# Routing attention and a cosine router: x divided while it is turned, routing in column strips, units in pairs

## The chip, the core and the metric

One core of a Trainium2 chip runs the whole kernel. TensorE (PE in the profile; its weight loads are PEld) multiplies and transposes into PSUM, VectorE (DVE), ScalarE (ACT) and GpSimd (POOL) work elementwise, SyncE (SP) issues most transfers. The metric is the device time of one execution in microseconds (us); less is better.

## The reference

Attention over B = 4 batches, H = 8 heads, S = 768 rows, D = 64 columns, in which a query sees only the keys whose nearest of C = 16 centroids is its own:

```python
mask = q_assign[:, :, :, None] == k_assign[:, :, None, :]
scores = np.where(mask, scale * np.matmul(q, k.transpose(0, 1, 3, 2)), -1000000000.0)
attn = np.exp(scores - np.max(scores, axis=-1, keepdims=True))
attn = attn / (np.sum(attn, axis=-1, keepdims=True) + 1e-09)
attn_out = np.matmul(attn, v)
```

Its output, as x of 3072 rows and 512 columns (8 heads side by side), goes to a router over 8 experts. A row's expert is the largest of its cosines with eight embeddings, its weight that expert's softmax, and the expert is two matrices with a relu between:

```python
xn = x / (np.linalg.norm(x, axis=-1, keepdims=True) + 1e-06)
logits = xn @ en.T / tau
expert_idx = np.argmax(logits, axis=1)
h = np.maximum(x[mask] @ w1[e], 0.0)
out[mask] = gate_w[mask, None] * (h @ w2[e])
```

## The kernel before

Heads are worked in 16 pairs (four batches of four). Both heads of a pair stand side by side in the 128 partitions. A pair has 12 units: two halves of the queries (hq, 384 each) times six blocks of 128 keys (j). Six units, one half, are a group: its outputs add up in one PSUM bank.

**A unit.** `scores` (line 326) makes turned scores, keys in partitions and 384 queries in columns, for both heads: first a product of one-hot assignments in bf16 (which adds a very large number where query and key share a centroid), then the fp32 product, each head in its own 64 rows of the array, into one of two `s_ps` buffers. `expo` (342) turns them on ScalarE into `prob` (4 buffers). `attend` (347) multiplies the values with `prob`, each head in its own 64 output columns, into `o_ps`, and VectorE adds `prob` into `acc`, of which the sum over partitions is the softmax's denominator.

**The end of a group.** `evict` (376) copies `o_ps` on ScalarE to `oT`, with a tiny constant `ev` per column added. `finish` (382) takes the denominators with 12 matmuls of one column (lines 391 to 397: six 128x128 pieces of `acc` are loaded as weights, each in two fp32 passes, and meet a column of ones), turns `oT` with three transposes (399), and VectorE divides while it copies to `xr`, x in rows, by reciprocals of 128x6 (401, 405).

**Preparation of the next pair.** `prep_pieces` (206) lists ten pieces: four turns of halves of q and k (three transposes each; q is copied on ScalarE, k on VectorE), products with the centroids (232), their transposes and the largest one per row (`assign`, 245 to 255, the last step on GpSimd), the sum of values (`mean`), the one-hot rows (`choose`, 261 and 262), and their transposes for q and for k (`turn_hot`, 274).

**Routing of a batch.** `route_pieces` (415) has eight pieces: for each of six row blocks four transposes of x (427), a copy on ScalarE, four accumulating matmuls whose moving side is eight columns of embeddings (437), a copy of the logits and a sum of squares (products on GpSimd at 424, the sum on VectorE at 445), and last `choose` (455), some twenty small operations and the transfer of the batch's x with its gate to DRAM (478).

**The order.** Inside the manual schedule (line 487) the program order is the order of TensorE's, VectorE's and ScalarE's queues. One step of the loop is a unit: scores and exponential of unit i + 1, the end of the last group at parts 0 and 1, one piece of preparation, attend of unit i, one piece of routing. All pieces take their PSUM from two banks (`misc`), so a piece also waits until the piece before the last has been copied out.

After the loop come the last batch's routing, the ranking of all rows by expert (lines 530 to 630, its first matmul at 536), and 28 blocks of 128 rows through the experts (633 to 734).

```python
                if i + 1 < len(units):
                    scores(i + 1)
                    expo(i + 1)
                if part == 0 and g > 0:
                    evict(g - 1)
                if part == 1 and g > 0:
                    finish(g - 1)
                if prepare:
                    prepare.pop(0)()
                if i < len(units):
                    attend(i)
                if routing:
                    routing.pop(0)()
```

Of the kernel before, what the change touches and what calls it, by code (L numbers as in the profile page):

```python
# [18 lines left out]
P = 128  # L19
# [16 lines left out]
def kernel(  # L36
# [43 lines left out]
    embT = const.tile([P, KD, E], F32, name="embT")  # L80
    prefc = const.tile([P, C], BF16, name="prefc")
    prefe = const.tile([P, E], BF16, name="prefe")
    ones = const.tile([P, 1], F32, name="ones")
# [20 lines left out]
    with ExitStack() as at:  # L104
# [41 lines left out]
        nc.vector.memset(cnB, 0.0)  # L146
        nc.vector.memset(cumx[:, 0], 0.0)
# [56 lines left out]
        nc.vector.tensor_copy(embT.rearrange("p c e -> p (c e)"), bk[:, 0 : KD * E])  # L204

        def prep_pieces(n):
# [86 lines left out]
            def mean():  # L293
# [10 lines left out]

            return [
                lambda: (turn("q", 0), values()),
                lambda: turn("k", 0),
# [4 lines left out]
                mean,  # L312
                choose,
                lambda: turn_hot(0, "q"),
                lambda: turn_hot(1, "k"),
            ]
# [7 lines left out]
        xr = {}  # L324
# [51 lines left out]
        def evict(g):  # L376
            n = units[GU * g][0]
            d = gr[g]
            d["oT"] = smp.tile([P, HS], F32, tag="oT", name="oT")
            nc.scalar.activation(d["oT"], d["o_ps"][:, 0:HS], ACTF.Identity, bias=ld[n]["ev"])  # L380

        def finish(g):
            n, hq, _ = units[GU * g]
            b, hp = pairs[n]
            d = gr[g]
            U = NJ // 2
            bk = misc()
# [12 lines left out]
            den = smp.tile([P, U, 2], F32, tag="den", name="den")  # L400
            nc.vector.reciprocal(den.rearrange("p u h -> p (u h)"), bk[:, HS : HS + 2 * U])  # L401
            if b not in xr:
                xr[b] = xp.tile([P, NJ, XW], F32, tag="xr", name="xr")
# [11 lines left out]
        def route_pieces(b):  # L415

            t = {}

            def turn(j):
                if j == 0:  # L420
                    t["sq"] = smp.tile([P, NJ], F32, tag="sq", name="sq")
                    t["lg"] = smp.tile([P, NJ, E], F32, tag="lg", name="lg")
                junk = smp.tile([P, DM], F32, tag="junk", name="junk")
                nc.gpsimd.tensor_tensor(junk, xr[b][:, j, 0:DM], xr[b][:, j, 0:DM], ALU.mult)  # L424
                bk = misc()
                for c in range(KD):
                    nc.tensor.transpose(  # L427
                        bk[:, P * c : P * c + P], xr[b][:, j, P * c : P * c + P], ident
                    )
                t[j] = trp.tile([P, DM], F32, tag="xT", name="xT")  # L430
                nc.scalar.copy(t[j], bk)
                t["junk", j] = junk

            def logits(j):
                bk = misc()
                for c in range(KD):
                    nc.tensor.matmul(  # L437
                        bk[:, 0:E],
# [339 lines left out]
```

## Time and profile before

| what | us |
|---|---|
| median of 3 runs | 970.41 (968.58 to 971.48) |
| profiled execution, its own time | 971.72 |
| its span, first to last instruction | 969.8 |
| PE busy in the span | 916.4 (94%) |
| DVE busy | 296.9 (31%) |
| ACT busy | 285.4 (29%) |
| POOL busy | 157.6 (16%) |

The span is what the rows of the profile lie in; 1.9 us of the profiled execution lie around it. A busy share is a mean over stages with different limits, so the stages are read apart. A line of the timeline gives the start, the time until the last of its instructions ended, engine, line, operation, tiles, shapes and count; on PE the starts are the safer reading, since the ends are modelled. An fp32 matmul is recorded as two passes, so `x4` at line 354 is one attend: two heads, two passes.

### The profile page before, as it was taken

How to read it: one execution, taken by the hardware profiler on the slowest of the kernel's cores; microseconds unless marked ns; L12 is line 12 of the kernel's file. 1: busy time of each engine (PE TensorE's matmuls, PEld its weight loads, DVE VectorE, ACT ScalarE, POOL GpSimd, SP SyncE). 2: the span in 40 equal slices, each digit the busy share in tenths (PEclk: the TensorE clock that was granted, in tenths of full speed). 3: DMA queues.
4: the chain of work that ended last, by engine and by line, in shares of the span. 5: the costliest groups of instructions: out<-in, count | busy, mean ns of one | idle time of the engine just before them, and what ended most of it. 6: DMA issues, size and time to landing. Idle time of an engine off the chain costs nothing.

```text
span 969.8 us, 13780 instructions
## 1 busy us (share of the span) xinstructions
PE 916.4 (94%) x5663; PEld 545.8 (56%) x5663; DVE 296.9 (31%) x527; ACT 285.4 (29%) x421; POOL 157.6 (16%) x195
## 2 busy tenths in 40 slices
PE   4999999999999999999996499999999999999996
PEld 2444446344464444544445477776776776776773
DVE  2545555554555546464553300000000000000000
ACT  3444443544445444444432011111111111111110
POOL 4011022201131111311012301011011011111110
PEclk9999999999999999999995599999999999999998
DMA  9722201420114111220000226256766573813710
GB/s 248 264 50 49 49 18 33 115 49 22 45 33 114 27 40 33 50 82 17 1 1 1 98 85 247 98 205 223 262 219 230 191 280 142 288 44 115 287 33 19
DMA packets 105648, 106.91 MB, mean 110 GB/s; under 512 B 77157, under 2 KB 77157, under 8 KB 105072
## 3 DMA queue, kind: packets, MB, share of 16 engines
q1 hardware_dynamic: 100928, 92.30, 30.1%
q0 software_dynamic: 4480, 13.65, 3.8%
q8 instruction: 47, 0.77, 0.3%
q14 instruction: 17, 0.14, 0.0%
q10 hardware_dynamic: 176, 0.05, 0.0%
HBM read 152.11 MB, written 13.64 MB: 171 GB/s over the span
## 4 chain that ended last, share of the span: by engine, by line
PE 48%; issue 25%; DMA 19%; DVE 5%; ACT 2%; POOL 1%; POOLq 0%; ACTq 0%; DVEq 0%
DMA out_dram<-y,sidx 19%; PE s_ps L334 16%; PE o_ps L354 14%; PE misc L391 5%; PE misc L217 3%; PE misc L437 3%; PE misc L427 2%; PE misc L274 1%; PE misc L232 1%; PE misc L399 1%; DVE oh L262 1%; PE misc L245 1%; DVE xr L405 1%; DVE pm L261 1%; DVE acc L373 1%
## 5 line engine op out<-in xcount | busy, mean ns | idle before, releaser
L345 ACT ACTIVATE prob<-s_ps 128x768 f32<-128x768 f32 x192 | 155.4, 811 | 245.1 <-PE s_ps L334 243.6
L682 PEld LDWEIGHTS h_ps<-xTm,w1s 128*128 128x128 f32 x1792 | 204.5, 193 | 19.9 <-DVE xTm L672 15.7
L682 PE MATMUL h_ps<-xTm,w1s 128*128 128x128 f32 x1792 | 208.6, 278 | 0.9 <-DMA w1s<-in_moe_w_dram 0.9
L695 PE MATMUL y_ps<-w2s,hT 128*128 128x512 f32 x448 | 201.2, 592 | 0.0
L354 PE MATMUL o_ps<-prob,v 128*64 128x384 f32 x768 | 166.3, 512 | 4.7 <-ACT prob L345 4.5
L334 PE MATMUL s_ps<-qT,kT 64*128 64x384 f32 x768 | 156.5, 486 | 0.0
L672 DVE COPY xTm<-x_ps 128x512 f32<-128x512 f32 x28 | 19.4, 691 | 378.4 <-PE x_ps L670 378.4
L373 DVE TENSOR_TENSOR acc<-acc,prob 128x768 f32<-128x768 f32 x128 | 125.3, 979 | 17.6 <-ACT prob L345 11.3
L695 PEld LDWEIGHTS y_ps<-w2s,hT 128*128 128x128 f32 x448 | 81.0, 190 | 81.3 <-issue 81.3
L689 ACT ACTIVATE hT<-h_ps 128x512 f32<-128x512 f32 x56 | 33.4, 597 | 240.5 <-PE h_ps L682 240.5
L704 POOL DMA_INDIRECT out_dram<-y,sidx x28 | 28.5, 1017 | 353.6 <-ACT y L703 347.7
L334 PEld LDWEIGHTS <-kH 64*128 64x128 bf16 x384 | 18.5, 93 | 103.4 <-issue 101.9
L334 PEld LDWEIGHTS s_ps<-qT,kT 64*128 64x128 f32 x768 | 70.2, 192 | 0.5 <-issue 0.5
L354 PEld LDWEIGHTS o_ps<-prob,v 128*64 128x64 f32 x768 | 38.0, 134 | 55.0 <-issue 36.3
L334 PE MATMUL s_ps<-qH,kH 64*128 64x384 bf16 x384 | 64.9, 335 | 0.9 <-ACT kH L282 0.9
L703 ACT ACTIVATE y<-y_ps,xin 128x512 f32<-128x512 f32 x28 | 19.2, 688 | 137.8 <-PE y_ps L695 131.6
L391 PEld LDWEIGHTS misc<-ones,acc 128*128 128x128 f32 x384 | 45.3, 191 | 17.9 <-issue 15.2
L391 PE MATMUL misc<-ones,acc 128*128 128x1 f32 x384 | 48.0, 252 | 0.4 <-DVE acc L373 0.4
L401 DVE RECIPROCAL den<-misc 128x6 f32<-128x6 f32 x32 | 6.3, 196 | 131.6 <-PE misc L399 131.6
L288 POOL TENSOR_TENSOR vs<-v 128x384 f32<-128x384 f32 x16 | 16.0, 998 | 187.7 <-DMA v<-in_v_dram 168.2
L424 POOL TENSOR_TENSOR junk<-xr 128x512 f32<-128x512 f32 x24 | 29.0, 1217 | 90.8 <-DVE sq L445 50.9
L255 POOL TENSOR_TENSOR sel<-sel,prefc 128x384 bf16<-128x384 bf16 x16 | 24.3, 1518 | 119.1 <-DVE sel L254 114.0
(144 smaller groups left out, 606.5 us busy)
## 6 DMA issues: line engine op xcount, KB each, us to landing
w1s<-in_moe_w_dram SPq DMA_DIRECT2D x30, 2048.0 KB
w2s<-in_moe_w_dram SPq DMA_DIRECT2D x30, 2048.0 KB
x_rows<-xr SPq DMA_DIRECT2D x4, 1539.0 KB
q<-in_q_dram SPq DMA_DIRECT2D x32, 192.0 KB
k<-in_k_dram SPq DMA_DIRECT2D x32, 192.0 KB
v<-in_v_dram SPq DMA_DIRECT2D x32, 192.0 KB
xin<-x_rows,gidx POOLq DMA_INDIRECT x28, 7.6
out_dram<-y,sidx POOLq DMA_INDIRECT x28, 7.8
```

Source lines behind the costliest of these rows:

```text
L217: nc.tensor.transpose(bk[:, P * j : P * j + P], t[nm][:, NJ // 2 * half + j].rearrange("p h d -> p (h d)"), ident,)
L334: nc.tensor.matmul(s_ps[:, h, 0:HS], lhsT=t[l][rows, P * j : P * j + P], rhs=t[r][rows, HS * hq : HS * hq + HS], start=first, stop=not first,)
L345: nc.scalar.activation(d["prob"], d["s_ps"][:, :, 0:HS], ACTF.Exp)
L354: nc.tensor.matmul(g["o_ps"][D * h : D * h + D, 0:HS], lhsT=ld[n]["v"][:, j, h], rhs=d["prob"][:, h], start=(j == 0), stop=(j == NJ - 1),)
L373: nc.vector.tensor_tensor(g["acc"], g["acc"], d["prob"], ALU.add)
L391: nc.tensor.matmul(bk[:, c0 : c0 + 1], lhsT=d["acc"][:, h, P * u : P * u + P], rhs=ones, start=True, stop=True,)
L424: nc.gpsimd.tensor_tensor(junk, xr[b][:, j, 0:DM], xr[b][:, j, 0:DM], ALU.mult)
L437: nc.tensor.matmul(bk[:, 0:E], lhsT=t[j][:, P * c : P * c + P], rhs=embT[:, c], start=(c == 0), stop=(c == KD - 1),)
L682: nc.tensor.matmul(bk[:, m : m + P], lhsT=w1s[j % 2][:, c, f0 + m : f0 + m + P], rhs=d["xT"][:, P * c : P * c + P], start=(c == 0), stop=( ...
L689: nc.scalar.activation(d["hT"][:, f0 : f0 + 512], bk, ACTF.Relu)
L695: nc.tensor.matmul(bk, lhsT=d["hT"][:, P * c : P * c + P], rhs=w2s[j % 2][:, c], start=(c == 0), stop=(c == KF - 1),)
L704: nc.gpsimd.indirect_dma_start(out=out[:], out_offset=bass.IndirectOffsetOnAxis(ap=sidx[:, j : j + 1], axis=0), in_=y, in_offset=None, bou ...
```

## The change

The ones that sum `acc` become a 128x64 matrix, so that one product per head (`total`) puts the denominator of each query into all 64 partitions of the head's output: it comes out turned, in the shape of `o_ps`. ScalarE copies it, VectorE takes the reciprocal of all 128x384 and multiplies it with `o_ps + ev` in one instruction into `xT`, x turned and divided (`divide`). Two parts later `rows` turns three blocks back and ScalarE copies them to `xr`. The router multiplies the turned x directly: four column strips (pairs of heads) times a 128x32 embedding each (8 columns and 24 of zeros) into the four quarters of one bank, then three transposes and one reduction over the strips. Squares are summed on ScalarE. The loop takes two units at a time: scores of two, a piece of preparation, attend of two, the sum and division of the last group at part 0, another piece of preparation, a piece of routing; the exponentials run a whole step ahead. Preparation has nine pieces, the first turns both q and k. `prob` has five buffers.

The diff, without the changes of sizes and of the embedding's copy at the top:

```diff
@@ -302,17 +305,17 @@
                 t["ev"] = smp.tile([P, 1], F32, tag="ev", name="ev")
                 nc.vector.tensor_copy(t["ev"], bk[:, 0:1])
 
+
             return [
-                lambda: (turn("q", 0), values()),
-                lambda: turn("k", 0),
+                lambda: (turn("q", 0), turn("k", 0), values()),
                 lambda: turn("q", 1),
                 lambda: turn("k", 1),
                 products,
                 assign,
-                mean,
                 choose,
                 lambda: turn_hot(0, "q"),
                 lambda: turn_hot(1, "k"),
+                mean,
             ]
 
 
@@ -321,7 +324,7 @@
         ngroups = len(units) // GU
         un = [dict() for _ in units]
         gr = [dict() for _ in range(ngroups)]
-        xr = {}
+        xr, xT = {}, {}
 
         def scores(i):
 
@@ -341,7 +344,7 @@
 
         def expo(i):
             d = un[i]
-            d["prob"] = pp.tile([P, 2, HS], F32, tag="prob", name="prob", bufs=4)
+            d["prob"] = pp.tile([P, 2, HS], F32, tag="prob", name="prob", bufs=5)
             nc.scalar.activation(d["prob"], d["s_ps"][:, :, 0:HS], ACTF.Exp)
 
         def attend(i):
@@ -373,84 +376,96 @@
                 nc.vector.tensor_tensor(g["acc"], g["acc"], d["prob"], ALU.add)
                 d.clear()
 
-        def evict(g):
-            n = units[GU * g][0]
+        def total(g):
+
             d = gr[g]
-            d["oT"] = smp.tile([P, HS], F32, tag="oT", name="oT")
-            nc.scalar.activation(d["oT"], d["o_ps"][:, 0:HS], ACTF.Identity, bias=ld[n]["ev"])
-
-        def finish(g):
+            bk = misc()
+            for h in range(2):
+                nc.tensor.matmul(
+                    bk[D * h : D * h + D, 0:HS],
+                    lhsT=ones,
+                    rhs=d["acc"][:, h],
+                    start=True,
+                    stop=True,
+                )
+            d["den"] = smp.tile([P, HS], F32, tag="den", name="den")
+            nc.scalar.copy(d["den"], bk[:, 0:HS])
+
+        def divide(g):
             n, hq, _ = units[GU * g]
             b, hp = pairs[n]
             d = gr[g]
+            if (b, hq) not in xT:
+                xT[b, hq] = xp.tile([P, NHP, HS], F32, tag="xT", name="xT", bufs=3)
+            nc.vector.reciprocal(d["den"], d["den"])
+            nc.vector.scalar_tensor_tensor(
+                out=xT[b, hq][:, hp],
+                in0=d["o_ps"][:, 0:HS],
+                scalar=ld[n]["ev"],
+                in1=d["den"],
+                op0=ALU.add,
+                op1=ALU.mult,
+            )
+            d.clear()
+
+        def rows(g):
+
+            n, hq, _ = units[GU * g]
+            b, hp = pairs[n]
             U = NJ // 2
             bk = misc()
             for u in range(U):
-                for h in range(2):
-                    c0 = HS + 2 * u + h
-                    nc.tensor.matmul(
-                        bk[:, c0 : c0 + 1],
-                        lhsT=d["acc"][:, h, P * u : P * u + P],
-                        rhs=ones,
-                        start=True,
-                        stop=True,
-                    )
-            for u in range(U):
-                nc.tensor.transpose(bk[:, P * u : P * u + P], d["oT"][:, P * u : P * u + P], ident)
-            den = smp.tile([P, U, 2], F32, tag="den", name="den")
-            nc.vector.reciprocal(den.rearrange("p u h -> p (u h)"), bk[:, HS : HS + 2 * U])
+                nc.tensor.transpose(
+                    bk[:, P * u : P * u + P], xT[b, hq][:, hp, P * u : P * u + P], ident
+                )
             if b not in xr:
                 xr[b] = xp.tile([P, NJ, XW], F32, tag="xr", name="xr")
-            c0 = 2 * D * hp
-            nc.vector.tensor_tensor(
-                xr[b][:, U * hq : U * hq + U, c0 : c0 + 2 * D].rearrange(
-                    "p u (h d) -> p u h d", d=D
-                ),
-                bk[:, 0:HS].rearrange("p (u h d) -> p u h d", h=2, d=D),
-                bc(den, [P, U, 2, D], 3),
-                ALU.mult,
-            )
-            d.clear()
+            nc.scalar.copy(
+                xr[b][:, U * hq : U * hq + U, P * hp : P * hp + P],
+                bk[:, 0:HS].rearrange("p (u w) -> p u w", w=P),
+            )
 
         def route_pieces(b):
 
             t = {}
-
-            def turn(j):
-                if j == 0:
+            U = NJ // 2
+
+            def products(half):
+
+                if half == 0:
                     t["sq"] = smp.tile([P, NJ], F32, tag="sq", name="sq")
                     t["lg"] = smp.tile([P, NJ, E], F32, tag="lg", name="lg")
-                junk = smp.tile([P, DM], F32, tag="junk", name="junk")
-                nc.gpsimd.tensor_tensor(junk, xr[b][:, j, 0:DM], xr[b][:, j, 0:DM], ALU.mult)
-                bk = misc()
-                for c in range(KD):
-                    nc.tensor.transpose(
-                        bk[:, P * c : P * c + P], xr[b][:, j, P * c : P * c + P], ident
-                    )
-                t[j] = trp.tile([P, DM], F32, tag="xT", name="xT")
-                nc.scalar.copy(t[j], bk)
-                t["junk", j] = junk
-
-            def logits(j):
                 bk = misc()
                 for c in range(KD):
                     nc.tensor.matmul(
-                        bk[:, 0:E],
-                        lhsT=t[j][:, P * c : P * c + P],
-                        rhs=embT[:, c],
-                        start=(c == 0),
-                        stop=(c == KD - 1),
-                    )
-                nc.vector.tensor_copy(t["lg"][:, j], bk[:, 0:E])
+                        bk[2 * C * c : 2 * C * c + 2 * C, 0:HS],
+                        lhsT=embT[:, c],
+                        rhs=xT[b, half][:, c],
+                        start=True,
+                        stop=True,
+                    )
+                t["pT"] = smp.tile([P, HS], F32, tag="asT", name="asT")
+                nc.scalar.copy(t["pT"], bk[:, 0:HS])
+
+            def logits(half):
+                bk = misc()
+                for u in range(U):
+                    nc.tensor.transpose(
+                        bk[:, P * u : P * u + P], t["pT"][:, P * u : P * u + P], ident
+                    )
                 nc.vector.tensor_reduce(
-                    t["sq"][:, j : j + 1], t["junk", j], axis=AXX, op=ALU.add
+                    t["lg"][:, U * half : U * half + U],
+                    bk[:, 0:HS].rearrange("p (u c e) -> p u e c", c=KD, e=2 * C)[:, :, 0:E],
+                    axis=AXX,
+                    op=ALU.add,
                 )
 
-            def both(j):
-                if j < NJ:
-                    turn(j)
-                if j > 0:
-                    logits(j - 1)
+            def norms(half):
+                for j in range(U * half, U * half + U):
+                    junk = smp.tile([P, DM], F32, tag="junk", name="junk")
+                    nc.scalar.activation(
+                        junk, xr[b][:, j, 0:DM], ACTF.Square, accum_out=t["sq"][:, j : j + 1]
+                    )
 
             def choose():
                 lg, sq = t["lg"], t["sq"]
@@ -480,7 +495,13 @@
                     in_=xr[b],
                 )
 
-            return [lambda j=j: both(j) for j in range(NJ + 1)] + [choose]
+            return [
+                lambda: products(0),
+                lambda: (logits(0), norms(0)),
+                lambda: products(1),
+                lambda: (logits(1), norms(1)),
+                choose,
+            ]
 
 
         prepare, routing = [], []
@@ -488,9 +509,12 @@
             for piece in prep_pieces(0):
                 if piece:
                     piece()
-            scores(0)
-            expo(0)
-            for i in range(len(units) + 2):
+            for m in range(2):
+                scores(m)
+                expo(m)
+
+
+            for i in range(0, len(units) + 6, 2):
                 g, part = divmod(i, GU)
                 if i < len(units) and i % (2 * NJ) == 0:
                     n = i // (2 * NJ)
@@ -507,23 +531,26 @@
                             nc.sync.dma_start(
                                 out=w2s[w], in_=moe_w2[0].rearrange("(c p) d -> p c d", p=P)
                             )
-                if i + 1 < len(units):
-                    scores(i + 1)
-                    expo(i + 1)
-                if part == 0 and g > 0:
-                    evict(g - 1)
-                if part == 1 and g > 0:
-                    finish(g - 1)
+                for m in range(i + 2, min(i + 4, len(units))):
+                    scores(m)
+                    expo(m)
                 if prepare:
                     prepare.pop(0)()
-                if i < len(units):
-                    attend(i)
+                if part == 4 and g > 0:
+                    rows(g - 1)
+                for m in range(i, min(i + 2, len(units))):
+                    attend(m)
+                if part == 0 and g > 0:
+                    total(g - 1)
+                    divide(g - 1)
+                if prepare:
+                    prepare.pop(0)()
                 if routing:
                     routing.pop(0)()
-                if part == 1 and g > 0 and g % (2 * NHP) == 0 and g < ngroups:
+                if part == 4 and g > 0 and g % (2 * NHP) == 0:
                     assert not routing
                     routing = route_pieces(g // (2 * NHP) - 1)
-            for piece in route_pieces(B - 1):
+            for piece in routing:
                 piece()
```

## Rows read from the trace of the kernel before

**Rows 1.** Busy time by stage: us, engines (instructions), granted clock, DMA share, GB/s

```profile
20.90:506.40 485.50, 476.58 (x3156) 225.84 (x3156) 252.36 (x414) 219.50 (x314) 80.41 (x95) 1.00 0.21 57
506.40:547.70 41.30, 19.32 (x115) 17.90 (x113) 18.13 (x54) 7.12 (x11) 13.00 (x14) 0.54 0.13 48
```

**Rows 2.** Timeline of the pair from 77.5 us, PE and two others

```profile
77.50 0.34 PE L334 MATMUL s_ps<-qH,kH 64*128 64x384 bf16 x2
...
78.41 0.87 PE L354 MATMUL o_ps<-prob,v 128*64 128x384 f32 x4
78.53 0.81 ACT L345 ACTIVATE prob<-s_ps 128x768 f32<-128x768 f32 x1 [0.84 <-PE s_ps L334]
...
82.30 1.50 PE L391 MATMUL misc<-ones,acc 128*128 128x1 f32 x12
...
83.66 0.53 PE L399 MATMUL misc<-ident,oT 128*128 128x128 f32 x3
...
84.02 0.49 PE L217 MATMUL misc<-ident,k 128*128 128x128 f32 x3
...
90.53 0.52 PE L232 MATMUL misc<-qT,cnB 128*32 128x384 f32 x2
...
91.31 0.87 PE L354 MATMUL o_ps<-prob,v 128*64 128x384 f32 x4
...
100.43 0.56 DVE L262 TENSOR_TENSOR oh<-sel,pm 128x384 bf16<-128x384 bf16 x1
...
101.05 0.51 PE L274 MATMUL misc<-identb,oh 128*128 128x128 bf16 x6 [0.23 <-DVE oh L262]
...
105.35 0.87 PE L354 MATMUL o_ps<-prob,v 128*64 128x384 f32 x4
...
106.15 0.34 PE L334 MATMUL s_ps<-qH,kH 64*128 64x384 bf16 x2
```

**Rows 3.** Timeline of PE at the start of the loop

```profile
20.95 0.50 PE L334 MATMUL s_ps<-qH,kH 64*128 64x384 bf16 x2 [0.89 <-ACT kH L282]
...
22.52 0.53 PE L334 MATMUL s_ps<-qH,kH 64*128 64x384 bf16 x2
```

**Rows 4.** Timeline of PE, first scores of pairs 4, 5 and 6

```profile
135.34 0.34 PE L334 MATMUL s_ps<-qH,kH 64*128 64x384 bf16 x2
...
172.37 0.34 PE L334 MATMUL s_ps<-qH,kH 64*128 64x384 bf16 x2
...
202.61 0.34 PE L334 MATMUL s_ps<-qH,kH 64*128 64x384 bf16 x2
```

**Rows 5.** Groups by line and shape, DVE: busy us, mean ns | idle before

```profile
L373 DVE TENSOR_TENSOR acc<-acc,prob 128x768 f32<-128x768 f32 x128 | 125.3, 979 | 17.6 <-ACT prob L345 11.3
...
L405 DVE TENSOR_TENSOR xr<-misc,den 128x384 f32<-128x384 f32 x32 | 17.9, 558 | 1.1
...
L471 DVE RECIPROCAL sq<-sq 128x6 f32<-128x6 f32 x4 | 0.8, 192 | 0.1
...
L182 DVE RECIPROCAL cn_r<-cn_r 128x1 f32<-128x1 f32 x1 | 0.2, 163 | 0.0
...
L182 DVE RECIPROCAL en_r<-en_r 8x1 f32<-8x1 f32 x1 | 0.1, 148 | 0.0
```

**Rows 6.** The same view, ACT

```profile
L240 ACT COPY asT<-misc 128x384 f32<-128x384 f32 x16 | 7.7, 480 | 2.5 <-PE misc L232 2.4
...
L469 ACT ACT_TABLE_LOAD x4 | 5.1, 1283 | 0.1
```

**Rows 7.** Timeline of PE, the last attend and the ranking's first matmul

```profile
505.70 0.20 PEld L354 LDWEIGHTS o_ps<-prob,v 128*64 128x64 f32 x4 [0.79 <-ACT prob L345]
...
529.69 0.33 PE L536 MATMUL misc<-cumx,onesb 128*128 128x200 bf16 x1 [3.57 <-POOL cumx L468]
```

**Rows 8.** Line 363: count, duration in ns (min/median/max), first and last start

```profile
L363 DVE SCALAR_TENSOR_TENSOR acc<-prob x32: 947/950/1791, 27.7 to 500.4; 128x768 f32<-128x768 f32 x32
```

More of the change, by code (lines that the diff above doesn't have):

```diff
@@ L79 @@
     cnB = const.tile([P, NHP, 2 * C], F32, name="cnB")
-    embT = const.tile([P, KD, E], F32, name="embT")
+    embT = const.tile([P, KD, 2 * C], F32, name="embT")
     prefc = const.tile([P, C], BF16, name="prefc")
     prefe = const.tile([P, E], BF16, name="prefe")
-    ones = const.tile([P, 1], F32, name="ones")
+    ones = const.tile([P, D], F32, name="ones")
     epsc = const.tile([P, 1], F32, name="epsc")
@@ L146 @@
         nc.vector.memset(cnB, 0.0)
+        nc.vector.memset(embT, 0.0)
         nc.vector.memset(cumx[:, 0], 0.0)
@@ L203 @@
             nc.tensor.transpose(bk[:, E * c : E * c + E], emb[:, P * c : P * c + P], ident[0:E, 0:E])
-        nc.vector.tensor_copy(embT.rearrange("p c e -> p (c e)"), bk[:, 0 : KD * E])
+        nc.vector.tensor_copy(
+            embT[:, :, 0:E], bk[:, 0 : KD * E].rearrange("p (c e) -> p c e", e=E)
+        )
         def prep_pieces(n):
@@ L388, in finish, with route_pieces @@
             for u in range(U):
-                for h in range(2):
-                    c0 = HS + 2 * u + h
+                nc.tensor.transpose(
+                    bk[:, P * u : P * u + P], xT[b, hq][:, hp, P * u : P * u + P], ident
+                )
+            if b not in xr:
+                xr[b] = xp.tile([P, NJ, XW], F32, tag="xr", name="xr")
+            nc.scalar.copy(
+                xr[b][:, U * hq : U * hq + U, P * hp : P * hp + P],
+                bk[:, 0:HS].rearrange("p (u w) -> p u w", w=P),
+            )
+        def route_pieces(b):
+            t = {}
+            U = NJ // 2
+            def products(half):
+                if half == 0:
+                    t["sq"] = smp.tile([P, NJ], F32, tag="sq", name="sq")
+                    t["lg"] = smp.tile([P, NJ, E], F32, tag="lg", name="lg")
+                bk = misc()
+                for c in range(KD):
                     nc.tensor.matmul(
-                        bk[:, c0 : c0 + 1],
-                        lhsT=d["acc"][:, h, P * u : P * u + P],
-                        rhs=ones,
+                        bk[2 * C * c : 2 * C * c + 2 * C, 0:HS],
+                        lhsT=embT[:, c],
+                        rhs=xT[b, half][:, c],
                         start=True,
@@ L397, in finish @@
                     )
-            for u in range(U):
-                nc.tensor.transpose(bk[:, P * u : P * u + P], d["oT"][:, P * u : P * u + P], ident)
-            den = smp.tile([P, U, 2], F32, tag="den", name="den")
-            nc.vector.reciprocal(den.rearrange("p u h -> p (u h)"), bk[:, HS : HS + 2 * U])
-            if b not in xr:
-                xr[b] = xp.tile([P, NJ, XW], F32, tag="xr", name="xr")
-            c0 = 2 * D * hp
-            nc.vector.tensor_tensor(
-                xr[b][:, U * hq : U * hq + U, c0 : c0 + 2 * D].rearrange(
-                    "p u (h d) -> p u h d", d=D
-                ),
-                bk[:, 0:HS].rearrange("p (u h d) -> p u h d", h=2, d=D),
-                bc(den, [P, U, 2, D], 3),
-                ALU.mult,
-            )
@@ L432, in turn @@
-                t["junk", j] = junk
-            def logits(j):
-                bk = misc()
-                for c in range(KD):
-                    nc.tensor.matmul(
-                        bk[:, 0:E],
-                        lhsT=t[j][:, P * c : P * c + P],
-                        rhs=embT[:, c],
-                        start=(c == 0),
-                        stop=(c == KD - 1),
-                    )
-                nc.vector.tensor_copy(t["lg"][:, j], bk[:, 0:E])
-                nc.vector.tensor_reduce(
-                    t["sq"][:, j : j + 1], t["junk", j], axis=AXX, op=ALU.add
-                )
@@ L449, in both @@
-            def both(j):
-                if j < NJ:
-                    turn(j)
-                if j > 0:
-                    logits(j - 1)
+                nc.vector.tensor_reduce(
+                    t["lg"][:, U * half : U * half + U],
[8 more added lines that the diff above has]
+                        junk, xr[b][:, j, 0:DM], ACTF.Square, accum_out=t["sq"][:, j : j + 1]
+                    )
```

4 lines of the change are left out of this document (removed).

## The prediction

> **What bounds the kernel now.** I read the stage table first [rows 1]. From 20.9 to 506.4 us (attention) TensorE is busy 476.6 of 485.5 us while VectorE has 252 and ScalarE 219.5; after 547.7 us stands the expert stage, which the change does not touch. So the question is what TensorE's queue does between 21 and 506 us, and how long the thin stretch to 547.7 takes, where TensorE was granted 0.54 of its clock.
>
> The timeline of one head pair comes next [rows 2]; its 12 units take 106.15 - 77.50 = 28.65 us. A unit's scores (S) start at 77.50, its attend (A) follows at 78.41: 0.91 us. From A at 105.35 to the next S: 0.80. S streams 0.16 us of bf16 and 0.64 of fp32 columns, A streams 0.64, so each leaves a gap behind it: 0.11 after S, 0.16 after A. The gap is not there when S follows S: at the start of the loop, where matmuls run at about half the speed (a record of 0.50 us against 0.34), S at 20.95 is followed by S at 22.52, 1.57 us, no more than twice its 0.80 of columns [rows 2, 3]. A directly behind A without another wait is not in the trace. I take the gap as the price of changing the shape of the array's tiles, paid once per run of one shape.
> The Trainium skill, TensorEngine Tiling (Array Packing), Key Properties, says that a change of tiling mode, not of the tile alone, drains the engine; by it A behind A would save its gap too, which no row here shows.
>
> A group (six units) ends with 12 one-column matmuls, 1.36 us (82.30 to 83.66), and three transposes, 0.36 [rows 2]. Routing a batch costs 37.03 + 30.24 - 2 x 28.65 = 9.97 us, over two pairs [rows 4], three times in the loop.
>
> **Part by part, per pair, on TensorE.**
> (a) Two units at a time: six SS and six AA instead of twelve of each save 6 x 0.11 + 6 x 0.16 = 1.62 us.
> (b) Group ends: before 2 x (1.36 + 0.36) = 3.44. After, the sum by the matrix of ones has A's tile shape and columns and stands right behind A: 2 x 0.64 = 1.28. The row transposes: 2 x 0.36 and one gap of 0.14, the other shared with the assignment's transposes (0.14 is what products lose, 0.78 against 0.64 of columns, 90.53 to 91.31 [rows 2]): 2.14 in all. Saves 1.30.
> (c) q and k of half 0 are turned together: about 0.2 less in gaps.
> Sum: 3.12 us less work per pair.
>
> (d) What the change adds is VectorE's reciprocal of 128x384, and its price is the unknown. The trace has RECIPROCAL of 6 elements at 192 ns and of one at 163 (128 partitions) and 148 ns (8 partitions) [rows 5]. The slope is 5.8 ns an element from the first, 8.8 from the second, 7.3 from their mean: 384 x 7.3 + 148 = 2.95 us, with ends at 2.4 and 3.5. I take 2.95; the operation is the same and neither end is nearer.
> The Trainium skill, VectorE: DVE Perf Modes, First, the fixed hardware budget, says that the reciprocal is an iterative divide with a repeat count of 8; at that page's 0.96 GHz it is by my estimate 3.35 us, which would make the sum below 7 us longer.
>
> (e) Who waits behind it. Set t = 0 at a pair's first S. SS 1.71, six transposes 0.84, AA 1.28, sum 0.64: to 4.47. A hand-over from TensorE takes 0.23 (S at 77.50 and 0.80 of columns, its exponential at 78.53), one from VectorE 0.06 (oh ends 100.99, its transposes start 101.05) [rows 2]. The copy on ScalarE, 0.48 [rows 6], ends at 5.18; reciprocal 5.24 to 8.19; the product with it, 0.56 as L405 [rows 5], to 8.78; only then, in VectorE's order, the copy of k's second half, to 9.26. The centroid products need that copy. TensorE reaches them at 4.47 + 0.16 + q 0.46 + SS 1.71 + k 0.48 + AA 1.44 = 8.72 and waits to 9.32: 0.60 us. Below 2.35 us of reciprocal this wait is gone.
> Products 0.78 and SS 1.71 bring TensorE to 11.81, the assignment's transposes to 12.17; two steps of 0.56 on VectorE to 13.55, two accumulations of 0.98 [rows 5] to 15.5 (they cover the GpSimd step between), two more of 0.56 to 16.55. The one-hot transposes want that result; TensorE is there at 12.65 + AA 1.44 + SS 1.71 = 15.80: 0.80 us of wait. Before, the same place cost 0.23 [rows 2].
> Per pair: 28.65 - 0.23 - 3.12 + 1.40 = 26.70, a saving of 1.95; 16 pairs 31, less 1 for the first, which has no group end ahead of it: **30 us**.
>
> (f) Routing. After: two products of 0.78, two sets of three transposes at 0.46, 2.5 us; the chain of some eleven small VectorE operations at about 0.2 us (as L471 [rows 5]) delays the next one-hots by some 1.4, other waits 0.2: 4.1 against 9.97. Three batches: **17.5 us**.
>
> (g) After the last attend. Before: the last A starts at 505.70, its columns end at 506.35, and the ranking matmul starts at 529.69 [rows 7]: 23.3 us. After: VectorE has four accumulations queued behind the last reciprocal but one, so the last sum starts about 2.2 us on; sum and copy to 3.6, reciprocal and product to 7.2, row transposes and products at half the clock to 9.3, copy and transposes to 10.8, three squares ahead of the second half's copy on ScalarE to 12.8, transposes and reduction to 14.4, choice 1.2, GpSimd's counts 1.6: 17.3. **6 us** saved.
>
> Sum: 53.5 us. The profiled execution took 971.7 (span 969.8), the median of the runs is 970.4; I take the 53.5 from the median: **917 us**.
>
> **Costed at nothing.** On ScalarE the copies of sums, rows and products (32, 32 and 8, at 0.48 [rows 6]) are 35 us and the 24 squares, at an estimated 0.7, 17 us: with what it has, 219.5 + 52 of 485.5 us [rows 1], and a unit's exponential now has a whole step of about 4 us until its attend; without that lead three squares in a row, some 2 us, would hold an attend. If the squares needed another table set, each batch half would pay two loads of 1.28 us [rows 6]: hidden in the loop, at most 5 us in the tail. Fifth prob buffer, third turned x, padded embedding: no instruction on a chain. x_rows goes out one pair later in SP's queue, behind the next pair's loads instead of ahead of them; those are a whole pair early. GpSimd loses its 24 products.
>
> **The rivals.** *Hidden reciprocal* (2.4 us or less): no wait at products, 16 x 0.6 and 0.6 in the tail: 907. For it: the slope from 128 partitions. *Dear reciprocal* (3.5): 0.58 more each time: 927; for it the other slope. *The gap is not of the shape*, so each S and A keeps it: 1.62 and 0.3 (the sums) come back, and the waits shrink by 0.55: 1.4 x 16, 939. Against it stands S behind S [rows 3], for it that A behind A is not seen. *VectorE becomes the bound, slower*: an accumulation of the same queue took 1.79 us instead of 0.95 [rows 8], and the long ones have GpSimd work beside them. Were every reciprocal stretched as much, to 5.9 us, the wait at products would grow by 1.35 up to a reciprocal of 4.3, and from there the row transposes of the second group wait too, two waits a pair: 17 x 1.35 + 33 x 1.6 = 76, 993 us. It decides from 5.2 us on (23 + 33 x 0.9 uses up the 53.5), 13 ns an element. Against it: GpSimd is busy 80 us in 485 [rows 1] and loses its largest product.
>
> **How the numbers follow.** Forecast 0.42, hidden 0.18, dear 0.20, gaps stay 0.15, VectorE bound 0.05. From 901 (hidden, with a little less wait at the one-hots) to 941 (gaps stay) all but the last and some unforeseen are in. Faster by over 0.3% (about what a measurement here tells from none) 0.95, slower 0.04, same 0.01.
>
> **What would show it.** Right: RECIPROCAL 128x384 near 2.95 us; S starts 0.80 apart inside a step and A 0.64; TensorE waits of 0.6 at products for kT and 0.8 at the one-hots for oh; pairs of 26.7 us; ranking some 17 us after the last A. Wrong: a reciprocal over 4.3 us, an A behind A at 0.80, exponentials that wait for prob, attends that wait for ScalarE.

## The result and the profile after

The changed kernel takes **923.9 us** (median of 4 runs, 923.1 to 926.4) against 970.9 for the kernel before on the same chip: ratio 0.951 [0.947, 0.956], 47 us faster. The forecast was 917 with a range of 901 to 941: direction and size held, 6.5 us of the 53.5 did not come. The profiled execution took 926.4 us, its span is 924.4 (before 969.8), so the two profiles differ by 45.4 us.

By stage, after: us, then busy time (instructions) of PE, PEld, DVE, ACT and POOL, granted clock, DMA share, GB/s. The first two rows answer to [rows 1]; the last three are stretches inside the first.

```profile
19.40:465.70 446.30, 420.01 (x2759) 192.86 (x2758) 314.35 (x383) 235.40 (x369) 55.05 (x75) 0.98 0.23 63
465.70:505.00 39.30, 12.09 (x73) 6.88 (x72) 19.14 (x47) 8.62 (x20) 8.91 (x10) 0.54 0.17 61
178.70:182.20 3.50, 3.50 (x16) 1.39 (x15) 1.42 (x2) 0.00 (x0) 0.00 (x0) 0.51 0.01 4
291.40:298.20 6.80, 6.14 (x28) 2.94 (x30) 2.71 (x5) 0.97 (x2) 0.00 (x0) 0.50 0.08 31
407.40:410.80 3.40, 3.40 (x12) 1.05 (x12) 1.42 (x2) 0.00 (x0) 0.00 (x0) 0.51 0.00 0
```

Attention went from 485.5 to 446.3 us. TensorE's idle time rose from 8.9 to 26.3 us in it, and VectorE is busy 62 us longer: TensorE's busy time fell by 56.6 us, the stage by only 39.2. New, behind the start of the loop, are three stretches in which TensorE got 0.50 of its clock, 1.2 instead of 2.4 GHz; before, this part of the stage ran at 1.00.

One pair on TensorE, after (timeline; start us, duration us, line; answers to [rows 2]):

```profile
73.00 0.34 PE L337 MATMUL s_ps<-qH,kH 64*128 64x384 bf16 x2
...
73.82 0.33 PE L337 MATMUL s_ps<-qH,kH 64*128 64x384 bf16 x2
...
74.72 0.55 PE L418 MATMUL misc<-ident,xT 128*128 128x128 f32 x3
75.19 1.51 PE L357 MATMUL o_ps<-prob,v 128*64 128x384 f32 x8
76.64 0.34 PE L337 MATMUL s_ps<-qH,kH 64*128 64x384 bf16 x2
...
80.50 0.81 PE L384 MATMUL misc<-acc,ones 128*64 128x384 f32 x4
81.25 0.55 PE L220 MATMUL misc<-ident,q 128*128 128x128 f32 x3
...
85.36 0.52 PE L235 MATMUL misc<-qT,cnB 128*32 128x384 f32 x2
...
86.36 0.34 PE L337 MATMUL s_ps<-qH,kH 64*128 64x384 bf16 x2
...
91.15 0.33 PE L337 MATMUL s_ps<-qH,kH 64*128 64x384 bf16 x2
...
93.38 0.51 PE L277 MATMUL misc<-identb,oh 128*128 128x128 bf16 x6 [1.26 <-DVE oh L265]
...
99.82 0.34 PE L337 MATMUL s_ps<-qH,kH 64*128 64x384 bf16 x2
```

A pair without routing (a plain pair in what follows) is 99.82 - 73.00 = 26.82 us (28.65 before). S follows S by 0.82 us. Two attends go from 75.19 to 76.64, 1.45 in all: 0.70 for A behind A (that is their distance in the trace), 0.75 for S behind A. The products last from 85.36 to 86.36, 1.00 us where they took 0.78 [rows 2]: 0.22 is the wait for k's second half. The one-hot transposes wait 1.26 us.

The same pair on VectorE and one row of GpSimd (timeline), and the reciprocal's group (busy us, mean ns):

```profile
81.88 2.55 DVE L400 RECIPROCAL den<-den 128x384 f32<-128x384 f32 x1 [1.18 <-ACT den L392]
84.46 0.62 DVE L401 SCALAR_TENSOR_TENSOR xT<-o_ps,ev,den 128x384 f32<-128x384 f32 x1
85.00 0.55 DVE L229 COPY kT<-misc 128x384 f32<-128x384 f32 x1
85.46 1.94 DVE L376 TENSOR_TENSOR acc<-acc,prob 128x768 f32<-128x768 f32 x2
...
89.73 2.53 DVE L376 TENSOR_TENSOR acc<-acc,prob 128x768 f32<-128x768 f32 x2
89.90 1.55 POOL L258 TENSOR_TENSOR sel<-sel,prefc 128x384 bf16<-128x384 bf16 x1 [7.06 <-DVE sel L257]
...
92.76 0.56 DVE L265 TENSOR_TENSOR oh<-sel,pm 128x384 bf16<-128x384 bf16 x1
```

```profile
L400 DVE RECIPROCAL den<-den 128x384 f32<-128x384 f32 x32 | 81.7, 2553 | 46.8 <-ACT den L392 46.8
```

The reciprocal is 2.55 us. The copy of k's second half stands behind it, as the prediction had it. Of the two runs of two accumulations, the second takes 2.53 us instead of 1.94: there GpSimd's product of `sel` (1.55 us from 89.90) runs beside them, and the one-hots stand behind.

A routed pair on TensorE and VectorE (timeline):

```profile
171.72 0.22 DVE L485 TENSOR_SCALAR sq<-sq 128x6 f32<-128x6 f32 x1 [0.37 <-ACT sq L484]
...
173.27 0.20 DVE L490 TENSOR_REDUCE mx<-lg 128x6 f32<-128x48 f32 x1 [0.74 <-ACT lg L489]
...
173.99 0.34 PE L337 MATMUL s_ps<-qH,kH 64*128 64x384 bf16 x2 [0.43 <-ACT prob L348]
...
178.49 0.62 PE L277 MATMUL misc<-identb,oh 128*128 128x128 bf16 x6 [2.71 <-DVE oh L265]
179.04 2.83 PE L357 MATMUL o_ps<-prob,v 128*64 128x384 f32 x8
```

Here the twelve small VectorE operations of the choice (170.22 to 173.91 us) make the one-hots wait 2.71 us, and then two attends take 2.83 us instead of 1.51: the half clock in the third row of the stage table. For 0.37 + 0.74 = 1.11 us of this chain VectorE itself waits, for the choice's square root and exponential on ScalarE, with a table load of 1.28 us ahead of each (the loads were there before the change too; no run leaves them out).

The tail, after the last attend (timeline; answers to [rows 7]):

```profile
465.01 0.81 PE L357 MATMUL o_ps<-prob,v 128*64 128x384 f32 x4
467.92 0.87 PE L384 MATMUL misc<-acc,ones 128*64 128x384 f32 x4 [2.09 <-DVE acc L376]
...
472.76 0.87 PE L418 MATMUL misc<-ident,xT 128*128 128x128 f32 x3 [3.98 <-DVE xT L401]
...
482.70 0.33 PE L563 MATMUL misc<-cumx,onesb 128*128 128x200 bf16 x1 [3.19 <-POOL cumx L483]
```

The last attend's first pass starts at 465.01, the ranking at 482.70: 17.7 us, against 24.0 [rows 7].

**Where the 45.4 us came from**, forecast and measured:

| part | forecast | measured | worked out from |
|---|---|---|---|
| start of the loop | 0 | 1.5 | first S at 19.42 instead of 20.95; 19.4 to 21.0 over all runs |
| pairs without their routing | 30 | 27.9 | 14 x 1.83, and 1.14 each in the first and last |
| routing in the loop | 17.5 | 11.3 | before 3 x 10.45 over plain pairs; after 6.27, 7.49, 6.33 |
| last attend to ranking | 6 | 6.3 | 24.0 and 17.7 |
| ranking to the end | 0 | -1.5 | 440.1 and 441.7 (unrounded: 1.54 apart); 438.6 to 443.0 in the eight other runs with as many expert tiles |

### The profile page after: what moved, and what is told of

Same layout as the page of the kernel before. It is cut to its first block, busy times and chain, and to the rows that moved or that the text cites. A ratio compares the mean times of both kernels' runs of the same rounds, so it can differ in the third digit from the quotient of the medians.

```text
span 924.4 us, 12733 instructions
## 1 busy us (share of the span) xinstructions
PE 847.7 (92%) x5207; PEld 497.6 (54%) x5207; DVE 358.7 (39%) x488; ACT 302.8 (33%) x485; POOL 127.9 (14%) x171
## 4 chain that ended last, share of the span: by engine, by line
PE 39%; issue 28%; DMA 19%; DVE 10%; ACT 2%; POOL 1%; SPq 0%; POOLq 0%; DVEq 0%
DMA out_dram<-y,sidx 18%; PE s_ps L337 15%; PE o_ps L357 13%; DVE acc L376 4%; PE misc L220 3%; PE misc L384 2%; PE misc L235 2%; PE misc L277 2%; DVE oh L265 1%; PE misc L418 1%; DVE sel L257 1%; DVE amax L256 1%; PE misc L440 1%; DVE pm L264 1%; PE misc L248 1%
## 5 line engine op out<-in xcount | busy, mean ns | idle before, releaser
L348 ACT ACTIVATE prob<-s_ps 128x768 f32<-128x768 f32 x192 | 153.4, 811 | 89.9 <-PE s_ps L337 67.7
L699 DVE COPY xTm<-x_ps 128x512 f32<-128x512 f32 x28 | 19.4, 691 | 379.7 <-PE x_ps L697 379.7
L357 PE MATMUL o_ps<-prob,v 128*64 128x384 f32 x768 | 148.9, 510 | 0.0
L376 DVE TENSOR_TENSOR acc<-acc,prob 128x768 f32<-128x768 f32 x128 | 130.2, 1017 | 5.8
L400 DVE RECIPROCAL den<-den 128x384 f32<-128x384 f32 x32 | 81.7, 2553 | 46.8 <-ACT den L392 46.8
L357 PEld LDWEIGHTS o_ps<-prob,v 128*64 128x64 f32 x768 | 47.3, 138 | 50.3 <-issue 48.7
L337 PEld LDWEIGHTS <-kH 64*128 64x128 bf16 x384 | 19.4, 94 | 58.2 <-issue 44.2
L392 ACT COPY den<-misc 128x384 f32<-128x384 f32 x32 | 15.3, 479 | 85.8 <-PE misc L384 85.8
L277 PE MATMUL misc<-identb,oh 128*128 128x128 bf16 x192 | 16.9, 227 | 27.2 <-DVE oh L265 27.2
L229 DVE COPY kT<-misc 128x384 f32<-128x384 f32 x32 | 17.7, 553 | 51.4 <-PE misc L220 51.4
```

The costliest lines, as they stand in the source:

```text
L277: nc.tensor.transpose(bk[:, P * j : P * j + P], oh[:, u, 2 * i + half].rearrange("p h c -> p (h c)"), identb,)
L337: nc.tensor.matmul(s_ps[:, h, 0:HS], lhsT=t[l][rows, P * j : P * j + P], rhs=t[r][rows, HS * hq : HS * hq + HS], start=first, stop=not first,)
L357: nc.tensor.matmul(g["o_ps"][D * h : D * h + D, 0:HS], lhsT=ld[n]["v"][:, j, h], rhs=d["prob"][:, h], start=(j == 0), stop=(j == NJ - 1),)
L376: nc.vector.tensor_tensor(g["acc"], g["acc"], d["prob"], ALU.add)
L400: nc.vector.reciprocal(d["den"], d["den"])
```

## The experiments

First the parts of the change, then the reciprocal, then what the loop still waits for.

**Old routing (e2).** The changed kernel with the routing of before (per row block four transposes, four matmuls of eight columns, and squares on GpSimd), shortened:

```
-                nc.tensor.matmul(bk[...], lhsT=embT[:, c], rhs=xT[b, half][:, c], ...)
+                nc.tensor.transpose(bk[...], xr[b][:, j, P * c : P * c + P], ident)
...
+                nc.gpsimd.tensor_tensor(junk, xr[b][:, j, 0:DM], xr[b][:, j, 0:DM], ALU.mult)
```

> The kernel after with the routing of before (turn x in rows again, four matmuls of eight columns per row block, squares on GpSimd and VectorE); loop, group ends and preparation as after, two buffers of turned x. Theory (the strips take work off TensorE's chain): a routed batch costs about 10 us in the loop instead of 6.7, and after the last attend the old pieces take some 12 us longer than the new: about 945 us. Rival (TensorE waits in those pairs anyway, so old routing pieces fill the waits): the loop's pairs cost the same and only the end is longer, 932 to 936 us.

942.3 us, ratio 0.968 [0.964, 0.973]. Plain pairs stay at 26.83 us; each batch's routing costs 8.3 us over plain pairs, and the last attend to the ranking takes 12.9 us longer than in the changed kernel. So the strips are worth 18.4 us, 12.9 of it in the tail and only 5 in the loop. Two things make the loop's part small: the changed kernel has its three stretches at half the clock there, e2 has none; and the old routing fills one wait of 1.26 us a batch (the pair from 155.8 us has no wait at the one-hots). That units two at a time alone make the old routing cheaper than its 10.45 is not shown: with the old group ends it costs 9.7 to 12.9 us a batch in e3 and 12.5 to 15.6 in e8, losses by the clock included.

**Units one at a time (e4).** The changed kernel with the order S, A, S, A, each S still a whole step ahead of its attend (shortened; the conditions at the loop's end are left out):

```
-                for m in range(i, min(i + 2, len(units))):
-                    attend(m)
+                attend(i)
+                scores(i + 3); expo(i + 3)
+                attend(i + 1)
```

> The kernel after with its two units taken in turn (S, A, S, A) while the exponentials keep their lead and all else stays in place. Theory (gap of the tile shape): each S and A leaves its gap again, 12 more gaps a pair, six of 0.10 and six of 0.08 to 0.16, of which the waits at products and one-hots swallow about a third: 12 to 18 us more, 936 to 942 us. Rival (the lead is what gains): within 3 us of 924.

946.5 us, 22.6 more than the changed kernel where 12 to 18 were expected: a plain pair is 27.90 instead of 26.83, some 16 us over the loop. Between the two profiled executions there are 19.9 us, and what is left of them lies at the loop's start (1.2), in the routing (1.5) and behind the ranking (1.2). TensorE (timeline):

```profile
77.25 0.34 PE L337 MATMUL s_ps<-qH,kH 64*128 64x384 bf16 x2
...
78.16 0.87 PE L357 MATMUL o_ps<-prob,v 128*64 128x384 f32 x4
78.96 0.34 PE L337 MATMUL s_ps<-qH,kH 64*128 64x384 bf16 x2
...
82.39 0.87 PE L357 MATMUL o_ps<-prob,v 128*64 128x384 f32 x4
83.08 0.82 PE L384 MATMUL misc<-acc,ones 128*64 128x384 f32 x4
```

S to A is back at 0.91 and A to S at 0.80, while the sum, which has other operands and another bank but A's tile shape, follows A by 0.69. So the gap comes with the change of shape; the rival that every S and A keeps it falls. That the lead of the exponentials is what gains falls too, for this run has that lead.

**Pairing alone (e3).** The kernel before with the new loop and order of pieces, group ends and routing left as they were (shortened):

```
+            for i in range(0, len(units) + 6, 2):
...
+                for m in range(i, min(i + 2, len(units))):
+                    attend(m)
```

> The kernel before with only the new loop: two units at a time, nine pieces in the new order, five prob buffers; group ends and routing as before. Theory (the gap is the price of changing the tile shape): S behind S at 0.80 and A behind A at 0.70, 1.5 us less per pair, partly paid back at the one-hots, some 20 us in all: about 950 us. Rival (pairing gains by the longer lead of the exponentials alone, which TensorE waited for only 4.5 us in all): 964 us or more.

967.0 us, ratio 0.994 [0.992, 0.997]: on the rival's side, but not for the rival's reason. S behind S is 0.82 and A behind A 0.70 there too. What gives the gaps back is one row of its timeline of TensorE:

```profile
96.82 0.51 PE L274 MATMUL misc<-identb,oh 128*128 128x128 bf16 x6 [1.58 <-DVE oh L262]
```

The one-hots wait 1.58 us instead of 0.23 [rows 2], and the loop has three stretches at half the clock. The new order of pieces is the suspect: it takes `mean` from ahead of `choose` and puts it last, so that one step fewer lies between the assignment and the transposes that want its result.

**Pairing with the mean in between (e8).** The same kernel with one line moved:

```
                 choose,
+                mean,
                 lambda: turn_hot(0, "q"),
                 lambda: turn_hot(1, "k"),
-                mean,
```

> The kernel before with units two at a time alone, and the group mean between choice and one-hots. Theory (pairing saves its gaps, and what gave them back was that the one-hots followed the choice directly): a pair of 26.8 to 27.0 us, no stretch at half the clock inside the loop, 940 to 945 us. Rival (the gaps are given back elsewhere, whatever the order): 960 us or more.

948.3 us, ratio 0.979 [0.976, 0.981]: 18.7 us faster than e3 by the order alone. A plain pair is 26.56 us, better than expected; the routed ones cost 12.8, 12.5 and 15.6 us a batch over plain ones, and the half clock stays, which was expected to go: four stretches, all in routed pairs (granted 0.51 from 305.6 to 309.0 us, 0.53 from 424.6 to 431.4). So pairing does save its gaps. Why the clock falls here is not shown: no wait of TensorE in the loop is longer than 0.64 us, and e2, with the same routing, keeps 1.00. Ahead of one stretch stand twelve matmuls of one column (from 182.25 us) and these (timeline of TensorE):

```profile
185.11 1.03 PE L436 MATMUL misc<-embT,xT 128*128 128x8 f32 x8 [0.64 <-DVE xr L404]
186.07 0.50 PE L333 MATMUL s_ps<-qH,kH 64*128 64x384 bf16 x2
```

**The changed kernel with the mean in between (e1).** The same line moved in the changed kernel.

> The mean piece moves between choose and the one-hot transposes; nothing else changes. Theory (the one-hot transposes of each pair are called one step too early): TensorE's 27.2 us of waits there, 16 of them, fall below 5; the three stretches of half the clock inside the loop (3.4, 6.8 and 3.4 us, which cost half of that) go with them, since the 2.7 us holds ahead of them are gone; a plain pair takes 25.5 us instead of 26.8, and the kernel about 894 us. Rival (VectorE's queue is nearly full, so a wait removed here shows up at the products, at a PSUM bank or at the next pair's scores): the other waits grow by 15 us or more and the time stays between 914 and 924.

**903.6 us**, ratio 0.928 [0.923, 0.933]: 20 us faster than the changed kernel. Behind the loop's first pair the one-hot transposes wait only in the three routed ones, 0.16 us each; a plain pair is 25.90 us, routing costs 3.3 us a batch, and the granted clock is 1.00 from 23.9 to 441.2 us. It stays some 10 us short of the theory, for the next wait appears (timeline of TensorE):

```profile
68.76 0.51 PE L277 MATMUL misc<-identb,oh 128*128 128x128 bf16 x6
...
71.04 0.34 PE L337 MATMUL s_ps<-qH,kH 64*128 64x384 bf16 x2 [0.33 <-DVE qH L283]
```

q's one-hots are now copied behind the reciprocal on VectorE, and the next pair's first S waits for them, 4.3 us over the loop; the products' 0.22 stays, some 3.5. (The place of `mean` in the kernel before, between assignment and choice, was not tried in the changed kernel.)

**Two copies on ScalarE as well (e7).** e1 with k's second half and q's one-hots copied by ScalarE:

```
+                elif half == 1:
+                    nc.scalar.copy(dst, bk[:, 0:HS])
...
-                    nc.vector.tensor_scalar(hot, bk[:, 0:S], BIG, None, ALU.mult)
+                    nc.scalar.activation(hot, bk[:, 0:S], ACTF.Copy, scale=BIG)
```

> The kernel with the group mean between choice and one-hots, and the copy of k's second half and the scaled q one-hots moved from VectorE to ScalarE. Theory (what that kernel still waits for is copies that stand behind the reciprocal on VectorE): a plain pair 25.3 us instead of 25.9, some 894 us. Rival (ScalarE's added copies delay exponentials and so attends): 903 us or more.

**895.7 us**, ratio 0.924 [0.923, 0.926], the fastest of all. A plain pair is 25.29 us, and the trace shows no wait of TensorE's matmuls in it. So what e1 still waited for were the two copies behind the reciprocal, 7.9 us in all; ScalarE had room.

**Without the division (e6).** The changed kernel multiplies by the sums; the reciprocal is left out.

```
-            nc.vector.reciprocal(d["den"], d["den"])
```

> The kernel after without the reciprocal: turned x is multiplied by the sums instead of their reciprocals, so the division is left out. Theory (the reciprocal is almost hidden): only the 0.21 us that the centroid products wait, 16 times, 2.55 in the tail and a little less in the routed pairs: 915 to 918 us. Rival (the order on VectorE is the bound, so that its 82 us of reciprocals move the one-hots too): 905 us or less.

970.0 us, which says nothing of the question: without the division x points elsewhere, the tokens choose other experts, and these take 31 tiles instead of 28 (groups of TensorE in e6 and in the changed kernel; 64 matmuls are one tile):

```profile
L708 PE MATMUL h_ps<-xTm,w1s 128*128 128x128 f32 x1984 | 232.1, 279 | 2.2 <-DMA w1s<-in_moe_w_dram 2.2
```

```profile
L709 PE MATMUL h_ps<-xTm,w1s 128*128 128x128 f32 x1792 | 208.2, 277 | 2.3 <-DMA w1s<-in_moe_w_dram 2.3
```

Up to the experts' first matmul the two can be compared: 491.4 against 500.6 us, 9.2 earlier; with the changed kernel's expert stage the span would be 915 and the time some 917, as in the theory. A plain pair is 26.61 us, 0.21 less: just the wait at the products, and the one-hots still wait 1.26. The tail is 5.8 us shorter, not 2.55: the last sum also no longer stands behind the last reciprocal but one.

**Two reciprocals (e5).** A second one, unused, ahead of the real one:

```
+            again = smp.tile([P, DM], F32, tag="junk", name="junk")
+            nc.vector.reciprocal(again[:, 0:HS], d["den"])
```

> The kernel after with a second reciprocal of 128x384, unused, ahead of the real one on VectorE. Theory (the timetable of the prediction: the reciprocal's time lands on the centroid products once they wait, and on the row transposes as well from 4.3 us on): two reciprocals last 5.1 us; (4.3 - 2.55) + 2 x (5.1 - 4.3) = 3.35 us more a pair, 16 pairs 54 us, and 2.6 in the tail: 975 to 985 us, slower than the kernel before. Rival (VectorE, busy 39% of the span, has room for it): within 10 us of the kernel after, at most 934 us.

981.0 us, ratio 1.012 [1.010, 1.014]: slower than the kernel before, by the theory's numbers. A pair is 30.26 us, 3.43 more (forecast 3.35). VectorE, then TensorE (timelines):

```profile
86.79 2.55 DVE L401 RECIPROCAL junk<-den 128x384 f32<-128x384 f32 x1 [1.18 <-ACT den L392]
89.38 2.55 DVE L402 RECIPROCAL den<-den 128x384 f32<-128x384 f32 x1
```

```profile
77.89 0.33 PE L337 MATMUL s_ps<-qH,kH 64*128 64x384 bf16 x2
...
79.63 0.55 PE L420 MATMUL misc<-ident,xT 128*128 128x128 f32 x3 [0.77 <-DVE ev L306]
...
90.28 0.52 PE L235 MATMUL misc<-qT,cnB 128*32 128x384 f32 x2
...
93.10 0.83 PE L235 MATMUL misc<-kT,cnB 128*32 128x384 f32 x2 [1.98 <-DVE kT L229]
93.87 0.34 PE L337 MATMUL s_ps<-qH,kH 64*128 64x384 bf16 x2
...
95.97 0.49 PE L420 MATMUL misc<-ident,xT 128*128 128x128 f32 x3
...
100.88 0.51 PE L277 MATMUL misc<-identb,oh 128*128 128x128 bf16 x6 [1.26 <-DVE oh L265]
```

The products last from 90.28 to 93.87, 3.59 us instead of 1.00: 2.59 more, the whole of the second reciprocal. (The 1.98 us in the row are only the idle part; the products of k's second half then run by themselves.) The row transposes of the pair's start come 1.74 us behind their S instead of 0.90, 0.84 more (0.77 of it in the row); those at 95.97 do not wait, and the one-hots wait as before: 2.59 + 0.84 = 3.43, where the theory has 2.55 + 0.80. (The profile puts the wait at L420 down to `ev`, a 0.15-us copy that ends just behind the turned x; what held them is the chain behind the reciprocal.) VectorE is busy only some 80% of the attention stage: its share says nothing here, its order does.

**No order of preference (e9).** The changed kernel without GpSimd's product of `sel`; ties between clusters are not broken, which is left out.

```
-                nc.gpsimd.tensor_tensor(sel, sel, bc(prefc, shp, 1), ALU.mult)
```

> The kernel after without GpSimd's product of sel with the order of preference (ties between clusters are then not broken, which is left out). Theory (the wait at the one-hots, 1.26 us instead of 0.80, is long because the two accumulations that run beside this product take 2.53 us instead of 1.94): they take 1.94 again, a plain pair 26.25 instead of 26.83, 16 pairs some 9 us, with up to 7 us more if the half clock inside the loop goes too: 907 to 916 us. Rival (the accumulations are slow for another reason, or the one-hots wait for something else): 920 us or more.

912.2 us, ratio 0.937 [0.933, 0.942], in the theory's range. VectorE and TensorE (timelines):

```profile
88.31 2.01 DVE L375 TENSOR_TENSOR acc<-acc,prob 128x768 f32<-128x768 f32 x2
```

```profile
91.44 0.51 PE L276 MATMUL misc<-identb,oh 128*128 128x128 bf16 x6 [0.74 <-DVE oh L264]
```

The accumulations are back at 2.01 and the one-hots wait 0.74 (forecast for the changed kernel: 0.80). Plain pairs are 26.31 us, routing costs 27.77 + 29.40 - 2 x 26.31 = 4.55 a batch, and nothing of the loop behind its start runs at half the clock.

## Why the prediction was right, and where it was off

**Bound.** Right: TensorE's queue sets the attention stage, and each wait forecast in it is where it was put.

**(a) Pairing.** Right in mechanism (e4). Sizes: S behind S 0.82 where 0.80 was taken, A behind A 0.70 where 0.64 was, so that six of each lose 0.48 us a pair; in return S behind A is 0.75, its gap 0.11 instead of 0.16, which gives some 0.30 back. The Trainium skill, TensorEngine Tiling (Array Packing), Key Properties, has the drain at a change of mode only; by it A behind A would be gapless. Here it keeps 0.06 of its 0.16.

**(b), (c) Group ends and turning.** Right in sum (the two were not measured apart): with the terms of (a) and (e) taken out (0.48 - 0.30 - 0.38 + 0.46), the rest of a pair is 0.14 us shorter than forecast.

**(d) Reciprocal.** Mis-sized: 2.55 us, not 2.95. The slope of the two 128-partition rows [rows 5], 5.8 ns an element, was the better; it gives 2.38. By the Trainium skill, VectorE: DVE Perf Modes, First, the fixed hardware budget, the estimate was 3.35; the measurement does not agree with it.

**(e) Waits behind it.** The timetable was right: products wait 0.22 for 0.60, which is the reciprocal's 0.40 less, and both of its thresholds fit: no wait at the products below 2.55 - 0.22 = 2.33 us (forecast 2.35), and, by e5, none at the row transposes below 5.1 - 0.84 = 4.3 (forecast 4.3). The one-hots wait 1.26 for 0.80. The step that failed is "two accumulations of 0.98 [rows 5] to 15.5 (they cover the GpSimd step between)": they do cover it, and it costs them 0.52 us (2.53 us beside it, 2.01 in e9 without it). That the errors of (a) to (e) nearly cancel is luck: 26.82 us a pair instead of 26.70, 27.9 over the loop instead of 30.

**(f) Routing.** This is the term that fell short, 11.3 us instead of 17.5. Before, it cost 10.45 us, not 9.97: the pair ahead of the two [rows 4] already had 0.5 of it. After, e9 gives 4.55 without a clock loss, near the forecast 4.1; the changed kernel pays 6.27 to 7.49. "The chain of some eleven small VectorE operations [...] delays the next one-hots by some 1.4" was right in size (2.71 against 1.26), but its consequence was not foreseen: behind that wait TensorE ran for 3.4 to 6.8 us at half its clock. Over three batches that is 1.7 + 2.9 + 1.8 = 6.4 us more than in e9, near half of the 13.6 us at half the clock, and about what the term fell short. The prediction read the clock for the tail alone.

**(g) Tail.** 6.3 us for 6. The squares on ScalarE needed no table load of their own; that bound was not needed.

**Rivals.** "Gaps stay" (939) falls by e4. "Dear reciprocal" (927) is nearest in time and wrong in cause. "Hidden reciprocal" falls too: it still costs 9 us (e6), more than half of it in the tail. "VectorE becomes the bound" did not come, but its mechanism is real: at 5.1 us of reciprocals (e5) the change takes 11 us more than the kernel before, so the turning point lies somewhat below the 5.2 of the prediction, which had counted on a larger gain.

**What it missed.** That the diff moves `mean` behind `choose` was in the timetable only as a slightly longer wait. It is the change's own loss: 20 us (e1). From 971 us the parts came, added in this order, as: pairing with the new order 4 (e3), new group ends 25 (e2), strips 18; `mean` ahead of the one-hots again, 20 more. In another order the shares differ: pairing is worth 22 us in e8 and 22.6 by e4.

## What to carry to other kernels

Where TensorE's queue is the bound and another engine's chain feeds it, put an unrelated piece between the end of the chain and the transposes that want it; one moved line was worth 20 us here, and without it the pairing alone kept 4 of its 22 us. Cost an operation on VectorE by what stands behind it in order, not by the engine's busy share: the first 2.55 us of reciprocal were nearly free in a pair, the next 2.55 cost 3.43. And add up waits in the loop's worst iteration, not only in the plain one.

## What was not expected of the hardware

- **The clock inside a busy loop.** Behind the 2.71-us wait TensorE's granted clock fell to 0.50 for 3.4 to 6.8 us, at three places in the changed kernel. The wait's length alone does not decide it: e5 has the same routed distance of 3.70 us from an S to the one-hot transposes, with a granted clock of 1.00 from 196.7 to 203.5 us behind it, and has 0.50 elsewhere (123.5 to 126.8 us), in a plain pair behind the same 1.98-us wait that other plain pairs have without a fall. In e8 it fell with no wait over 0.64 us. What decides stays open.
- **GpSimd beside VectorE.** Of the two accumulations beside GpSimd's 1.55-us product the first takes 0.95 us, the second 1.48; without the product 2.01 for both (e9). The product loses time as well: all its runs in the loop take 1.55 us, and the one at 15.2 us, with no accumulation beside it, 0.91 (durations in ns, min/median/max, in the changed kernel):

```profile
L258 POOL TENSOR_TENSOR sel<-sel,prefc x16: 908/1552/1558, 15.2 to 431.9; 128x384 bf16<-128x384 bf16 x16
```

The Trainium skill, SBUF — State Buffer, SBUF: two separate sides, has a lock between a VectorE operation with two inputs in SBUF and a GpSimd operation that reads SBUF; the rows agree: the second accumulation ends at 92.26, 0.8 us behind GpSimd's product (91.45), as if it had waited for it, and the product as if it had waited for the first.
